# One broadcast read of reciprocal row sums, issued as two reads, one for each head of a pair

## The chip, the cores and the metric

The kernel runs on one core of one Trainium2 chip. The metric is the device time of the whole program in microseconds (us): for the kernel before, the median of 3 timed runs is 762.94 us (761.92 to 763.22). One further execution was profiled; its rows are the ones shown below.

## The reference

Two batches, eight heads, 768 tokens, head dimension 64. Each query and key is hashed to 6 sign bits by a shared projection; a query attends only to keys with the same bits. Two feed-forward layers with fixed weights (512 to 2048 to 512) follow, all in float32:

```python
mask = q_bucket[:, :, :, None] == k_bucket[:, :, None, :]
scores = np.where(mask, scale * np.matmul(q, k.transpose(0, 1, 3, 2)), -1e9)
attn = np.exp(scores - np.max(scores, axis=-1, keepdims=True))
attn = attn / (np.sum(attn, axis=-1, keepdims=True) + 1e-09)
x = np.matmul(attn, v)                       # then to [1536, 512]
h = x @ w_in;  x = where(h >= 1, h, where(h <= -1, 0, (h + 1)**2 / 4)) @ w_out
h = x @ w_in2; out = (h - np.tanh(h)) @ w_out2
```

## The kernel before

**Attention.** Heads are taken in pairs, and a pair's queries in two halves of 384 (`SH`). For a block of 128 queries TensorE writes the scores over 768 keys into PSUM (`emit_s`, L447 and L451, tile `ss`); VectorE takes the row maximum (L465) and two small scalars from it (L468, tile `sm`); ScalarE takes the exponential with its row sum (L469, tile `p`, sums in `ls`); `p` is split into two float16 parts (L474 to L476, tile `phl`), which SyncE's queue turns by DMA transposes into `pt` (L480). After the six blocks of a pair (three for each head), TensorE multiplies `pt` with the values into `pv` (L571). The result is not yet divided by the row sums.

**The division.** `pv` has the two heads' 64 output dimensions on its 128 partitions and the 384 queries along the row, while the row sums lie with the queries on the partitions. They have to be turned and repeated: row `rb[h*64+d, q]` must hold `1/sum` of head `h`, query `q`, for all 64 `d`. In the first batch TensorE does that by matmuls (L510, copied by L515). In the second batch (`if b:` in `scale_l`) it goes through memory: VectorE forms the reciprocals (L493, L495), TensorE turns them (L498) into 6 rows of 128, VectorE copies these to `rts` (L499), a DMA stores them as `rsum` in DRAM (L500, 3 KB), and another DMA reads `rsum` back with every head's 384 values repeated on 64 partitions (L502, 192 KB, tile `rb`). This happens 8 times, once for each pair and half of the second batch. Then `pv` is multiplied by `rb` (L578 on VectorE), and the product is split into two parts `xh` (L239) and `xl` (L245) for the first feed-forward layer.

**Feed-forward.** Units of matmuls (`mats`, L737; L725 for the last) take `xh` and `xl`, or `gh` and `gl` of the hidden layer, against weights `wh` and `wl`; `post` evaluates the results. The first batch's units are mixed into the second batch's attention. The second batch's first layer begins when its last pair is divided.

**What sets the order.** Every operation is registered with a plan, with the cells it reads and writes. A table (`SCHEDULE`, compressed text) gives the order in which all of them are issued and the engine where there is a choice. Each engine works through its own instructions strictly in that order. All DMAs, transposes included, are issued by SyncE (SP) one after another; the issue of one waits if its data or its buffer isn't ready, and everything behind it waits too.

The lines of the transfer in question:

```python
src = rsum[m].rearrange("j k p -> j (k p)").unsqueeze(1).to_broadcast([2, D, SH])
one("SP", 400.0, lambda: SP.dma_start(out=RB[0], in_=src), [("rs", m)], [("rb", 0), ("rb", 1)])
```

The outermost dimension of this source is the head (2), then the 64 repeats with step zero, then 384 contiguous values.

Of the kernel before, what the change touches and what calls it, by code (L numbers as in the profile page):

```python
# [22 lines left out]
SCHEDULE = (
    "c-rk)dvH|c6+h>D-siruo84qL31O3vm?sI@L_=N#LIS}MNGymTPahb;2Vy`$(J~fAp@^eGZO1az4z0D?q1Eaij-##4sMSuZwsf32YPJ2N9mkFx|Iq2V3(}Be"
    "^HAutGn`58y?ej&oyYIIzTKsRw=aP!5Y}DI-0POX^-)-Saqm{O$y8S`Erf#xGISANwz=XG+qj82s2$fea6MRaOuqyngL8lvmqmD(11p$r2SSj@L&%-uMhzCQ"
    "wS*=Ng_=UB^%o5ghOC^=K4rkSTk*(E7R1aDkNgwxZ~p067!0C5?oT8xhj(mMS;=1o&^+7%C3i%lS&|k0>iJyzc^1p#@)dyJ80Im=&bb;oqzizE4lLH#*w}~-"
    "tDvh39^eg-64~s0*e=S2D6ea5WVHx2b9G1Ut{L+{btJ)^Et{I4K(rP^>MEYBIUk1NaRyiyvubM-iD+(Bydqj&9<}22F(}Dyh@@(Y;*qN9sdzPnD~+s3cG-E6"
    "(qw5Q!ph65tEYu@a9T-TIGhX@g)QdCl0d)^!CXf}M4C>1z6=Hp9muh)5atHMVKWd3nZaNnWM*T;^_u}7`V*nWE`sB893`WX?9an-9?mjC*|AT!<}CRm>AJxn"
    "v)}_CBDn9l%8A7y>i$SXSpY%9@4wrxIP7J>OmG~O&H*J4;^xgJ8U}1*j0vTlhzSs3>*$~mz?fgkhd*=IeeQl&GTUCYV!cgVtOjmFDVN`(5tqsiuG-t%yOaXC"
    "opsEfEnZXVl@@WCd<n3=p08d#*ueS9TDD>hW6MA0D_ytZ$PtdFVVX=MTZs4HFNAvN;KA>x!-qOatN!9XHg_)^lymmTmb;zj91Ph3`#FlD@vQL});_iUNei*s"  # L30
    "*mlE_qeqORi2Sqf{gAHWnnPDVSi_}!P#8kIeV_XF2C?st;+;Rd@y0%--rl=ch_}?sFTd^s$pyUd0%ssrqCoy!06*q1_$;`;_!Nl#^0N;<`1>(aTwnk^t{#K;"
    "<k8t6-h5Mt+3;I<%VfsyfYKNnl!_^oFV+COq=1PRyV;AJ!!yrl&7NYvL;+?v903-JJPsHL;1~XsNWr77-yi(zKV1964=tbXqxXH5^)7$U=lkT{2mbuN?@!!1"
    "?l{~$e%t~@P^VZ{mbN&5?KS_a+}8hc97li1!9g2<A}u&RO~|81Li`wi|Kv}p5FdS=X~rChk63|_6%63h5BU%MI!Za=W>LwS2c%El1;SLOA<Z91*e{jZ@qjw8"
    "Q#=6sZ`NGF(6;amk_ESfgb<r<y^V41qnx^(EJ7+)4QiVpph%^-=o0KVjFOE8-^3{?w7$ZJ`9h+#hf>+HA_D9UK|rNeH#OeTpb%y*fqLFqUCn3CoEe&N<zTC>"
    "sM2k1dA#ca)eTK^o0{Z3jParrPqO@4SSAFP_aihDm9eri*27pyF+g#si1Yg9%5Wf%msQIB6%`e^oF_S4?Y6iDrAbNsCsh!KxWRLHtg<o+vp8?2lxD@1Gb9ux"
    "142wIDne0sc`}tkmPb10)H6&ZlqxUJE6B-fif6|VvXjXOgr{3oeO5j<{a`GZ##mG-7S3Thkgauv&!-1mp;$t)MT>;4f&$0VV5l4?$V}lg41-w&pcc8gb323+"
    "lP#@L9%_n2EKBf@lGIIu;QriSSy>6f4V1Zp%_)K6)?&siOXZ|eP%m`?XZa4+)z#GcAQt0Kik_aHK-pp<-~gQqZ|=mRF12+l$HKNYmm$cus}dXW%D7?3da1D1"
    "##O88>MjAZs)|?Qz|eI!uq`+A`;@x2v~=_4QqBjFEjVz1U7_`1A@=@c^)YcwtN~MTiuSHuckR+r${n{*Shovi96s#u2dNXNd!;^b;2O>Lf$Wedn8|TBu2c7}"
    "Ie@FFrx^F#GkD21!`O3Uz%cNeE<bpX^J6;&4n9T+Ou1w{^5}ZGd$-<mUE6K9?Ur)WrcILMsG%XXfB*h_EHpV2d-iMu($3jNWINf8eLEQ39b)3neRnb;IOmLA"
    "yBia?--5e#BIc-DZl<EV3AWz97-AP*zh%po;ziIS_N)xoLm{WCy$oR8T7Ye!ZX7Z}t&-O(2nVyI7;L6=hQ3mSg|KD~T@)1Ba{2Ok)8Vr9?QCrXuo>2_bz~hZ"  # L40
    "@B|@bWi4(u;Z@$l<suNm?r!XA95DMkFJ?=YRO_Pt{!N=9Z%NxleSJO6Q~@Zgd6!};#aHlfR9i+n7_AJJHDA~Ov4ymMek4|7CKBynBX!;zjq^2)9^fLCqGEGl"
    "2Iea_s{(^E2BIXpxHxV?KH+MbIp;BqPLl`<4aQ<i6wdbL&hSYYO{(d(9S+MZ8UTT^GF3WF^I|S%PIq}I6mt^P355*lha>j1q|TBdInChyc--;(bF?k&r4dzV"
    "UCE=N9?<bXAS9ykIJ8TMwHw^g=J^~9^!x2Zf}Hoq{QhjTEXNUzw$?r^oPq*J1%pA0Cuzbk-GtI;gnZZ4b@|cynU)=+(h0SjW)fg?p{aKp9@W{lX=KMM<3>DE"
    "MxV1oGC!Y8Qw8&P&iDIGnLWfbDKHtM-52;$-*Ouo>fH@<>ldVUcF$QmYks@d<ujXIeeJbYPfv?x&FZQn4O-vcXw7+XR{J5#`bMiZYnHNVuo}_qF-59-)-2xH"
    "y`EZX=dxw1R;{LT9T*ru=99Pfqa*BMabc0@?xysZ={TEqbvXU~PUZJ2`<$VhHaJ@^HGSYNw7~3wfdR1A4p_`oD_6EtELxvv?QUsVpj2Pyyvua&rE`_Kq-TXv"
    "s*B5kb#lPp@29{owd~&B-bLFsQpKAK%x>PZ#<njt7Ob?eYkptf+K!H1rrLW@wzc;5O1V_dgT?dbUI5hjp^b=USW^>kZ%KFQdY9&uAQP~Xv01ZNRTYTRQsPx5"
    "bP6k_S}!bMNt*S7#q(HhZb3l-HN_~kbDCWc%z|h%1fg)q4`5q9r1O(Ol>pwq^6JpFEGbRXpu++J1IwaQ04nOz94(+zp%%(}MiW4Q*M$jH#b_il+6<bxoD16F"
    "jSonZ@J0y<p~^?jt@IL06Dg!w<H>R8uxZkWqtOjCw@qS}-sn!7MY@quMRH=o6Dm3Put|?aptFte$kSz{*T_+lK^qAa&pd6?S%gXOc&Xu0S1}}Y7RmzpoR&nY"
    "JdKQd=btnXB*+F0NZnPE+2k+X$*eRAv;dL`uYaPq?zK9an`9;tl_~eY_Dloq*+nnSllX%t2)#`*{nj8ar7O`s0U5oeEp*;SuhJFuJ~A^cm7z{!K~{NidaT3?"
    "RCa<qBQ~!Bh46{A1>`!pK)nULJRrRUoo5l5=!M18l}6PQl@5XT?8R1iQ6j9UohdqU(Kga`0@1WN9&vJ=7`31S0<EP1^`ygzSlYyDFfUA=GW0Tsdq|`gIi~G^"  # L50
    "w953&!yD+h>Nwzdcfc>7PTpZ+az@-oeso5z+9z-J2toF#r7s_bUx)G8!&dCk>!YMjY0aK+*O{RSHQ<@mXQlt9Ksf4p7RdY>e&du_5GT0{$9jP$-(yC@@f72i"
    "4CWNE7@^oWbs3wC({3YQkGF;H#>vYl4&#i3)fhv#F)0)OON9U9^3KsYXwMFba}b=Pb99dWANoF?ex@309N^i|dse*pY6n}yGi*Cfif=NfWt_wZJk1ZB<oAuQ"
    "<mhP-pZKml)$j}xftex0uag8gu}?U)nBtT|Gj@=M`HxdEZXC6la$ua@I64*ZE9b)aDTR}*9vs(Fz=;9E46ft2RXO>5!?D<LGS1+Cz7^wSTM16m>r+BUWHXN2"
    "38$Fs6U)w!M3}iq@bnntSLltWcN3giL&MBPia2hajj|0VPJl^f9gYMJCzq)>a)KjH=r(3T9j8*9I7%E&zUapZNG6YQg1(ItsGV@mPcS)fvLgT|S4-m~Fd=}W"
    "Qx(VdCBtC{aX8P&AMY|dd)nN`jPf#JI=ZwGGldvOXJ)3u>DYE)CctnE0b@Lk3GQ$JFmr#y%q;@PjLvYq6Tvo?iI|}ajGREDey7E;Ou;e0I7{?zk;J4U"
)


# [866 lines left out]
```

## Time and profile before

| | |
|---|---|
| timed runs | 762.94 us median, 761.92 to 763.22, 3 runs |
| profiled execution | 766.08 us, of which the span from first to last instruction is 764.2 us |
| TensorE (PE) busy | 739.8 us, 97% of the span |
| VectorE (DVE) busy | 543.0 us, 71% |
| ScalarE (ACT) busy | 450.9 us, 59% |
| GpSimd (POOL) busy | 344.5 us, 45% |
| mean granted TensorE clock | 0.993 |

How to read it: TensorE is busy nearly all the time, so the other engines' shares matter only where they make TensorE wait. An idle time is told with what ended it: "PE ss L447 <- ACT p L469" is TensorE standing before line 447 until ScalarE had finished line 469. The granted clock is 1.00 at TensorE's full 2.4 GHz and 0.50 at 1.2 GHz. The part of the span that belongs to the second batch's attention runs to about 494 us; behind it there are only feed-forward units.

### The profile page before, as it was taken

The numbers are of one execution on the slowest core, as the hardware profiler recorded it, in microseconds if no ns is written. First come the engines' busy times: TensorE is split into PE (matmuls) and PEld (weight loads), VectorE is DVE, ScalarE is ACT, GpSimd is POOL, SyncE is SP. The second block draws the span as 40 slices with busy tenths as digits, with TensorE's granted clock in tenths as the row PEclk, the third lists the DMA queues.
The fourth block names the chain that finished last, engine by engine and source line by source line (L and its number), as shares of the span: only waits on it lengthen the run. The fifth ranks groups of instructions, "written<-read, shape, count | busy, mean of one in ns | idle before, by whom it ended". The sixth has DMA issues, their size and how long they took to land. (4 is left out here: it accounts for less than half of the span.)

```text
span 764.2 us, 12558 instructions
## 1 busy us (share of the span) xinstructions
PE 739.8 (97%) x4608; PEld 685.9 (90%) x4608; DVE 543.0 (71%) x958; ACT 450.9 (59%) x728; POOL 344.5 (45%) x229
## 2 busy tenths in 40 slices
PE   7899999989999999999999998899999999999997
PEld 6666789768989999999999997799999999999997
DVE  7999988879888888987888895352633555253653
ACT  8998898878879688766775575052423324221110
POOL 6974465665646356555444576222013322231220
PEclk9999999999999999999999999999999999999999
DMA  6996886999999998997988867431221221122212
GB/s 191 212 283 232 204 254 233 222 214 249 246 226 235 198 207 205 269 212 212 232 226 222 198 165 127 121 111 58 81 69 56 69 69 56 56 59 67 69 41 83
DMA packets 164861, 124.97 MB, mean 164 GB/s; under 512 B 126864, under 2 KB 134848, under 8 KB 164800
## 3 DMA queue, kind: packets, MB, share of 16 engines
q1 hardware_dynamic: 164800, 124.18, 64.7%
q8 instruction: 36, 0.59, 0.3%
q14 instruction: 25, 0.20, 0.1%
HBM read 73.53 MB, written 19.95 MB: 122 GB/s over the span
## 5 line engine op out<-in xcount | busy, mean ns | idle before, releaser
L245 POOL TENSOR_TENSOR wl<-wr,wh 128x512 fp32r<-128x512 f32 x77 | 107.1, 1393 | 176.0 <-ACT wh L239 71.9
L737 PE MATMUL mm<-xh,wh 128*128 128x384 f32 x512 | 137.5, 339 | 1.8 <-DVE xh L239 1.8
L737 PE MATMUL mm<-xl,wh 128*128 128x384 f32 x512 | 136.3, 336 | 0.5 <-POOL xl L245 0.5
L737 PE MATMUL mm<-gh,wh 128*128 128x384 f32 x504 | 136.4, 341 | 0.0
L737 PE MATMUL mm<-xh,wl 128*128 128x384 f32 x512 | 136.1, 336 | 0.0
L737 PE MATMUL mm<-gl,wh 128*128 128x384 f32 x504 | 133.9, 336 | 0.0
L737 PE MATMUL mm<-gh,wl 128*128 128x384 f32 x504 | 133.9, 336 | 0.0
L475 POOL TENSOR_TENSOR phl<-p,phl 128x768 f16<-128x768 f32 x46 | 80.7, 1755 | 73.5 <-ACT phl L474 39.4
L245 POOL TENSOR_TENSOR gl<-tmp,gh 128x768 fp32r<-128x768 f32 x35 | 68.0, 1945 | 93.0 <-DVE gh L239 58.6
L469 ACT ACTIVATE p<-ss,sm 128x768 f32<-128x768 f32 x78 | 77.2, 989 | 39.7 <-DVE sm L468 37.0
L737 PEld LDWEIGHTS mm<-xh,wh 128*128 128x128 f32 x512 | 92.7, 189 | 4.0 <-DVE xh L239 2.1
L737 PEld LDWEIGHTS mm<-gh,wh 128*128 128x128 f32 x504 | 90.9, 189 | 4.0 <-issue 2.0
L737 PEld LDWEIGHTS mm<-xl,wh 128*128 128x128 f32 x512 | 93.4, 188 | 1.0 <-POOL xl L245 0.8
L239 ACT ACTIVATE wh<-wr 128x512 fp32r<-128x512 f32 x88 | 54.7, 625 | 66.1 <-PE mm L737 60.0
L737 PEld LDWEIGHTS mm<-xh,wl 128*128 128x128 f32 x512 | 93.6, 189 | 0.0
L465 DVE TENSOR_REDUCE sm<-ss 128x1 f32<-128x768 f32 x82 | 78.2, 954 | 20.6 <-PE ss L451 18.2
L737 PEld LDWEIGHTS mm<-gl,wh 128*128 128x128 f32 x504 | 92.1, 189 | 0.0
L737 PEld LDWEIGHTS mm<-gh,wl 128*128 128x128 f32 x504 | 92.1, 189 | 0.0
L246 DVE TENSOR_TENSOR wl<-wr,wh 128x512 fp32r<-128x512 f32 x67 | 50.4, 755 | 24.2 <-ACT wh L239 23.1
L787 DVE TENSOR_TENSOR accs<-mm,accs 128x768 f32<-128x768 f32 x45 | 43.0, 954 | 34.4 <-PE mm L737 34.1
L756 ACT ACTIVATE tmp<-mm,cb 128x768 f32<-128x768 f32 x32 | 28.8, 899 | 52.6 <-PE mm L737 52.6
L760 ACT ACTIVATE tmp<-mm 128x768 f32<-128x768 f32 x32 | 25.9, 809 | 53.7 <-PE mm L737 48.7
(179 smaller groups left out, 1235.0 us busy)
## 6 DMA issues: line engine op xcount, KB each, us to landing
w<-in_w SPq DMA_DIRECT2D x64, 512.0 KB
qr<-in_qT SPq DMA_DIRECT2D x32, 192.0 KB
wr<-scr0i SPq DMA_DIRECT2D x24, 256.0 KB
wr<-scr0o SPq DMA_DIRECT2D x24, 256.0 KB
krs<-in_kT SPq DMA_DIRECT2D x14, 384.0 KB
vr<-in_v SPq DMA_DIRECT2D x12, 384.0 KB
scr0i<-wr SPq DMA_DIRECT2D x16, 256.0 KB
scr0o<-wr SPq DMA_DIRECT2D x16, 256.0 KB
```

What stands on the lines that cost most here:

```text
L239: ways = [("A", ca, lambda: A.activation(dst, src, AF.Copy)), ("V", cv, lambda: V.tensor_copy(dst, src), 1)]
L245: op([("G", cg, lambda: G.tensor_tensor(dst, src, hi.bitcast(F32), op=ALU.subtract)), ("V", cv, lambda: V.tensor_tensor(dst, src, hi.bitca ...
L246: ("V", cv, lambda: V.tensor_tensor(dst, src, hi.bitcast(F32), op=ALU.subtract), 1)], reads, writes)
L465: one("V", 870.0, lambda: V.tensor_reduce(z[:, 0:1], s, axis=AX.XY, op=ALU.max), cell, [c])
L469: one("A", 970.0, lambda: A.activation(halves(p), s, AF.Exp, bias=z[:, 2:3], scale=z[:, 1:2], accum_out=LS[lm][:, lk:lk + 1]), cell + [c], ...
L475: lo = [("G", 1600.0, lambda: G.tensor_tensor(hl[:, S:2 * S], p, hl[:, 0:S], op=ALU.subtract)), ("V", 870.0, lambda: V.tensor_tensor(hl[:, ...
L737: T.matmul(ps[:, s + hf, 0:SH], m[:, kc * 128:(kc + 1) * 128], y[:, hf * SH:(hf + 1) * SH], start=(kc == 0 and i == 0), stop=(kc == 3 and ...
L756: one("A", 690.0, lambda: A.activation(halves(t), ps, AF.Relu, bias=half_b, scale=0.5), [pc], [c])
L760: one("A", 690.0, lambda: A.activation(halves(t), ps, AF.Tanh), [pc], [c])
L787: one("V", 870.0, lambda: V.tensor_tensor(a, ps, a, op=ALU.add), [pc], c)
```

## The change

The read at L502 becomes two reads, one for each head. Each has 64 partitions of `rb` as its destination and, as its source, the head's 384 values with 64 repeats as the outermost dimension. Each writes one of the two cells `rb`. The plan gets 8 operations more, and the table is written anew for their number.

```diff
 SCHEDULE = (
-    "c-rk)dvH|c6+h>D-siruo84qL31O3vm?sI@L_=N#LIS}MNGymTPahb;2Vy`$(J~fAp@^eGZO1az4z0D?q1Eaij-##4sMSuZwsf32YPJ2N9mkFx|Iq2V3(}Be"
...
+    "c-rk)d2pRo*?*qrtnYf?yXGeMCTWsp>6WBPnuUg}lr{@(x{zQ?TLKoaB@`@`E-ba8LKjgBYAb372bDoZ)IrC=QD<;O9lmcwM^SMZT+s0kN5*l+@nb&EdlR8e"
...
-                src = rsum[m].rearrange("j k p -> j (k p)").unsqueeze(1).to_broadcast([2, D, SH])
-                one("SP", 400.0, lambda: SP.dma_start(out=RB[0], in_=src), [("rs", m)], [("rb", 0), ("rb", 1)])
+                for h in range(2):
+                    src = rsum[m][h].rearrange("k p -> (k p)").unsqueeze(0).to_broadcast([D, SH])
+                    one("SP", 400.0, lambda h=h, src=src: SP.dma_start(out=RB[0][h * D:(h + 1) * D], in_=src), [("rs", m)], [("rb", h)])
```

SyncE's queue near the seventh and the eighth of these reads, before (`wr` are weights, `scr` their copies in DRAM, `out_T` the output):

```order
L685 DMA scr1o_245<-wr_119 128x512
L502 DMA rb_102<-rsum_161 128x1x384
L480 DMA_TRANSPOSE pt_108<-phl_106 128x12x128
L480 DMA_TRANSPOSE pt_109<-phl_107 128x12x128
L480 DMA_TRANSPOSE pt_109<-phl_106 128x12x128
L659 DMA wr_119<-scr0i_185 128x512
L480 DMA_TRANSPOSE pt_109<-phl_107 128x12x128
L500 DMA rsum_162<-rts 6x128
L792 DMA out_T<-accs 256x1x384
L659 DMA wr_118<-scr0i_184 128x512
L502 DMA rb_102<-rsum_162 128x1x384
L659 DMA wr_116<-scr0i_186 128x512
```

The same place after (lines below the edit have moved by one):

```order
L686 DMA scr1o_245<-wr_119 128x512
L503 DMA rb_102<-rsum_161 64x384 x2
L480 DMA_TRANSPOSE pt_108<-phl_106 128x12x128
L480 DMA_TRANSPOSE pt_109<-phl_107 128x12x128
L480 DMA_TRANSPOSE pt_109<-phl_106 128x12x128
L660 DMA wr_119<-scr0i_185 128x512
L480 DMA_TRANSPOSE pt_109<-phl_107 128x12x128
L500 DMA rsum_162<-rts 6x128
L793 DMA out_T<-accs 256x1x384
L660 DMA wr_118<-scr0i_184 128x512
L503 DMA rb_102<-rsum_162 64x384 x2
L660 DMA wr_116<-scr0i_186 128x512
```

The second read stands right behind the first; nothing else has changed its place, here or at the other six reads. On TensorE, VectorE, ScalarE and GpSimd the instructions stand in the same order as before.

## Rows read from the trace of the kernel before

**Rows 1.** Page, part 1; then the chain of waits: start, us, what.
```profile
PE 739.8 (97%) x4608; PEld 685.9 (90%) x4608; DVE 543.0 (71%) x958; ACT 450.9 (59%) x728; POOL 344.5 (45%) x229
...
494.69 261.01 PE mm L737 x1491
```

**Rows 2.** Waits over the span: total us, times, longest us.
```profile
DVE rb L578 <- DMA rb<-rsum: 9.8, 4, 4.3
...
PE ss L447 <- ACT p L469: 5.6, 8, 2.2
...
PE mm L737 <- DVE xh L239: 1.8, 1, 1.8
```

**Rows 3.** Four stretches: length, busy us and count by engine, clock, DMA share, GB/s.
```profile
230.00:470.90 240.90, 240.89 (x1487) 229.87 (x1485) 203.27 (x351) 170.76 (x281) 133.01 (x85) 1.00 0.90 210
473.19:477.64 4.45, 4.45 (x16) 4.45 (x17) 3.13 (x6) 2.86 (x5) 2.50 (x2) 0.62 0.38 71
493.61:498.00 4.39, 3.93 (x12) 3.60 (x13) 1.56 (x3) 1.75 (x2) 2.24 (x2) 0.61 0.01 4
498.00:755.70 257.70, 257.70 (x1483) 256.49 (x1483) 123.69 (x161) 74.59 (x97) 65.45 (x42) 1.00 0.22 67
```

**Rows 4.** Timeline at the seventh read: start, us, instruction, count, [idle before <-releaser].
```profile
466.91 0.96 DVE L465 TENSOR_REDUCE sm<-ss 128x1 f32<-128x768 f32 x1 [2.91 <-PE ss L451]
...
470.46 0.51 PE L737 MATMUL mm<-gh,wl 128*128 128x384 f32 x2
...
471.09 0.56 DVE L578 TENSOR_TENSOR rb<-pv,rb 128x384 f32<-128x384 f32 x1 [3.23 <-DMA rb<-rsum]
...
472.06 0.99 ACT L469 ACTIVATE p<-ss,sm 128x768 f32<-128x768 f32 x1 [5.57 <-DVE sm L468]
...
473.19 0.62 PE L447 MATMUL ss<-ak,aq 128*128 128x384 f32 x2 [2.22 <-ACT p L469]
```

**Rows 5.** Timeline at the eighth read.
```profile
485.25 0.55 SPq L502 DMA_DIRECT2D rb<-rsum  x1
...
487.92 0.43 DVE L239 CAST wh<-wr 128x512 fp32r<-128x512 f32 x1 [1.69 <-DMA wr<-scr0i]
...
491.46 0.34 PE L737 MATMUL mm<-xh,wh 128*128 128x384 f32 x1
492.61 0.56 DVE L578 TENSOR_TENSOR rb<-pv,rb 128x384 f32<-128x384 f32 x1 [4.26 <-DMA rb<-rsum]
...
493.61 0.44 PE L737 MATMUL mm<-xh,wh 128*128 128x384 f32 x1 [1.81 <-DVE xh L239]
493.64 1.00 POOL L245 TENSOR_TENSOR xl<-rb,xh 128x384 fp32r<-128x384 f32 x1 [9.62 <-DVE xh L239]
...
494.69 0.69 PE L737 MATMUL mm<-xl,wh 128*128 128x384 f32 x1 [0.46 <-POOL xl L245]
```

**Rows 6.** Stretches of the clock, columns as in rows 3.
```profile
156.65:159.95 3.30, 3.30 (x21) 1.72 (x22) 2.81 (x6) 2.10 (x5) 1.64 (x1) 0.50 0.89 208
474.05:477.40 3.35, 3.35 (x12) 3.35 (x11) 3.06 (x5) 1.89 (x5) 2.50 (x2) 0.50 0.37 70
494.55:497.90 3.35, 3.21 (x10) 3.21 (x11) 1.46 (x3) 1.75 (x2) 1.32 (x2) 0.50 0.00 0
```

**Rows 7.** DMA issues: sizes.
```profile
rb<-rsum SPq DMA_DIRECT2D x8, 192.0 KB
```

**Rows 8.** Stretches in which one transfer moves most of the bytes, columns as in rows 3.
```profile
468.00:469.00 1.00, 1.00 (x8) 1.00 (x7) 0.00 (x0) 0.00 (x0) 1.00 (x2) 1.00 0.14 40
469.00:470.00 1.00, 1.00 (x8) 1.00 (x7) 0.00 (x0) 0.00 (x0) 0.47 (x1) 1.00 0.15 41
478.00:479.50 1.50, 1.50 (x10) 1.50 (x10) 0.75 (x2) 0.74 (x1) 0.00 (x0) 1.00 0.86 215
```

**Rows 9.** SyncE's issues: one by one at the seventh read; then min/median/max ns.
```profile
464.44 0.55 SPq L502 DMA_DIRECT2D rb<-rsum  x1
465.09 4.09 SPq L480 DMA_TRANSPOSE pt<-phl  x1
...
L502 SPq DMA_DIRECT2D rb<-rsum x8: 541/546/1429, 218.2 to 485.2; - x8
...
L480 SPq DMA_TRANSPOSE pt<-phl x72: 1274/1628/4881, 20.0 to 479.8; - x72
```

More of the change, by code (lines that the diff above doesn't have):

```diff
@@ L23 @@
 SCHEDULE = (
-    "c-rk)dvH|c6+h>D-siruo84qL31O3vm?sI@L_=N#LIS}MNGymTPahb;2Vy`$(J~fAp@^eGZO1az4z0D?q1Eaij-##4sMSuZwsf32YPJ2N9mkFx|Iq2V3(}Be"
-    "^HAutGn`58y?ej&oyYIIzTKsRw=aP!5Y}DI-0POX^-)-Saqm{O$y8S`Erf#xGISANwz=XG+qj82s2$fea6MRaOuqyngL8lvmqmD(11p$r2SSj@L&%-uMhzCQ"
-    "wS*=Ng_=UB^%o5ghOC^=K4rkSTk*(E7R1aDkNgwxZ~p067!0C5?oT8xhj(mMS;=1o&^+7%C3i%lS&|k0>iJyzc^1p#@)dyJ80Im=&bb;oqzizE4lLH#*w}~-"
-    "tDvh39^eg-64~s0*e=S2D6ea5WVHx2b9G1Ut{L+{btJ)^Et{I4K(rP^>MEYBIUk1NaRyiyvubM-iD+(Bydqj&9<}22F(}Dyh@@(Y;*qN9sdzPnD~+s3cG-E6"
@@ L28 @@
[L28 to L55, printed above, removed]
+    "c-rk)d2pRo*?*qrtnYf?yXGeMCTWsp>6WBPnuUg}lr{@(x{zQ?TLKoaB@`@`E-ba8LKjgBYAb372bDoZ)IrC=QD<;O9lmcwM^SMZT+s0kN5*l+@nb&EdlR8e"
@@ new lines @@
+    "a+8}1j?DDjd*An*_nh;b-?N<Ociy}0w&U;?+zWg5lXpn%ghMG98y8pJp>Gp(voATJA|JnxuI9-41hR~U7_nUMdWB#QTEZ6~qJztURVP`30acYdnE<i~nf?;5"
+    "Tt`Vkr<<@awmOCi+C&l(q8RBFei-ab@~{nQE5;!44}3XNi51Z(s@)OD{OTpAq+YII7W@!;k_>9zTT~P$V2hqDw!iaTq*Mmjb3f7e^~=|44IsQ;Am&3SjA+32"
+    ";dX4>4(s47YlBvvq7FF3m+|E-9Uat+1dW%e{-*nC*FcZ#s{-M!UJd2EyBb>ev8u)nIFiW_U~@~_Zps#wG-Ov46)#&>WVdG0P?Ks)HZE?-B<m|P4UlMBq2tNa"
+    "lBLPIWW1tA$7xA@eOWY7Q(m3Lns{X#m&CNsBXRJhNZZ1TTcR`?&FDx_Y{zXZi6*Rgkc?T;AZ|rcnDio6;A12k8}Sfa-<5)_R3iC*@e+!sV@d_7ztCcOOn5Ob"
@@ new lines @@
+    "N;dq?NAQ0Oo-B6LN%`Sq5`+a&9f_QbNCqbe$hW{n;hvG=A>3=B2DO_VAfZS;!6C&HkJ&eIt|1_LSp40)?iKIjf}EXv*EZYcv=S8Ik*!CBLb=&EU-rJUcR<Q+"
+    "5Y*Y%$^S<_E4%ph;+ZyrYggUOu3@c=u3ouqoVLEq{q5u}|0F}}tgVSjJR@-M!<@^HJ@7I4(5W+g4F~n$8e%6voa(zzbe(j+>0-<Y9Q+1a_>}$}HhuLFK4D>l"
+    "KDZwre)M7W=s%Es;xov_t$1eQbR!euG}rv6A5tH@p1+^}jQ`*l&;Q_l`O}l~1b<$A?>YWm9|Ys@G$Z&H-+?B2zZu|P7~J#}cwhM&fP4wQWWjHK^QB8PJpK}V"
+    "UVaw3Ulh*+|1rOm!*lQxi}a7cDn)2VSu9a}dnLd#5{Q4}=@ELG!Bd(PeU-k39PC6<0w|Vx954v*|07+z3%pN7A}{~R3;yW*!S?+>{?51U7uj!p|F188<oAyE"
@@ new lines @@
+    "!Y`Tq>z_Lgd%*@tL~Rsjk_GyIBkWm6ecyFoan+w0pyL>%1e)R3KnUbS_&DcZ#uu3NIDY1NgTNz!pSFXTjX~sFACG+W8B77Xwi9*ml<-f2F}k+25c;zp1R>>J"
+    "XXV|e`C0hLor*~~c>BSGpy>V>=eO{Cj}ePR5ZOHv$!Kq)<uLGY{c#}x^_5#{^&ZXC%?yQ7Z}YK?3+K2~j5b)ilPvCPdMn8L`g>%z97Sk?R<^d0H8)Q*G{x#C"
+    "den*r)my^`dslbM0qE@P7xxpf>New`%Ce>g7-I~!bT0$y+_aRIbWkl|bxSR<Snp!iS|3d`v!FB{)UIHxm{ry71;3(eX|)07RPfd;WLc9gVa4@nSj9Q8PFBn6"
+    ">uM!LMWvuci}#31T3o@(STiF*jlC_UN@dCxEiEl6Eh(x7fK*iqnnvw-d3pUJdxOoaN*^?l%u*r|OB-XXP!Z*gdVI5_tf2K=)kC>!t1M{gMQw_3Qi@B97?&j_"
@@ new lines @@
+    "-0e^I^av+)DT}UVaf_KW$bTONFVfHe*%kZ=FS^v@)L&Z*UUxOQirU+uxK*Iau8KU^(z3ES0>yH}hS>6=;Z3knz`*)}BglsC7&=>Xhz)>bm8=KAfzDpBXHOR2"
+    "meHbBNNg6@;LesEEh}wkU{}>^d^>H~zi*$v55=u@b$jb*!bH&SQ-kz@PpBKX9RI=z{-k)4kK4-ZM|Je5I3bUi7!eN(=T3oiK!22-aZWSaR`h^4b&I0+OXv^7"
+    "&|>%=l-E8mehRHqJ56S}`hACQ()!qe;9iZ2yAQGl*pqj2oNyUFW+UoP?|QF(L>%9D&pr2wZh6aIahDMzAKZQLl(au^|Lrz1I(}RMBYwjKA-$9Crn~Mp87y&<"
+    "(=q-&&KSL$?nS&cd*oes^lmIcdF0MCiaX%;(}zk%V8d<uYu4|BE86+7?NG%K@J0adI=B`NgFJW$#!blXH&m5K2p*Z>og9{IG^2(9#>a<Xr-TYeY+X|cH|*-A"
@@ new lines @@
+    ">yqGOCtNF<uK_+7%7S?R#^>S|uwZxt12N1m;R79`*4i!GXmg_)8@qKQRF!U?xT<#(Z5+OINFwJp?rdYN$!$!f!0NM955ZfyHndAf4*_4dD7Dfr>raOp+XT-6"
+    "lVsXKa$Z4^7HFnAC~u4?jH7@^QEd^guFinQ(mF?FY_$Z_Xtt$96P{^_8~u{ib-qYf3t8njA|A(>1;Ns#a!G|^HB2;Bd0DeJ%S4oMF5>Eulv|+^qN2)<2^M6t"
+    "UcgI~<6h~eRHd_<EwW<6DTpRSkj_G;PeO5@<y#Kt9X10fFLx4tsqgW?<-VVAJal=Wbc?SRCAch&am!-9#zhKE!np+6%RJ?_lohqwk;b*Qo$^!^^xLbBfmLCt"
+    "c5Q3dw(N9iL#d^+DJ`m0jY_F#ytMMD2-Zc{29_u~NXk_X$)L+h1d%qnuf5f8y?#w=+u)I1gZ-=4^=Z9acdc~X?qR)`1|OYJm$u)e-=m$&o@rmz_mH#I>CyJe"
@@ new lines @@
+    "E2$Bj4z$<Xt)g{s6~AWP(5@W-Y~9wKjBn>-bakM%jFB(Ntq~*D;(&<@#+oj7-MvT0E^`~UJmR{C-Q^>@4q5Nm37$7>Qr=YqFbei{qc&M`N1t)V)}HP!b`Qv|"
+    "LAhz|<u|I4@ikKJki%C?Il#o&E-@C22Ea#MZ`0<HJ2!H74>|U*J+zChx14bYheo&GXb%jm*|bKF5cXZ64AovGH>~TrVh}bCfP(%G!|Hv!tGnAU6z}Wi5%SxF"
+    "*DZwM5o%zXtzygSml>K`W)g&`6>O<dqLP&_rYb5Yb2iIl5z7&v2$IF7nSx{t(($51G!Ah9H*m-|sZfJ7S80w_GNe$KYt6MHCd@`4v?MBl<{)Uo!7^?}VW<_%"
+    "7SSdsh50eCNg8635Ym+)H$=<)Afyt&Fm!=Hp%H=1$b)bl2HfB?%r796LEzw2gPD{twGMI?LIRHF3>V&V;tT_rnpwwC)Ra6!0A?snVv@jejepgF$l#MXc%TiP"
@@ new lines @@
+    "nbg9y8Dq$Zg>6HNpt(Y$FENM0rDRSq$M^tEk~O+d$qN?`(V31=1+XMjW|F~y8pBxz15K$1IcO%&<{*SxPd+u%wK<)HN!2#bO)WRy0wXjOz)+edQb<N7JDRfs"
+    "3JTkkwg9jJCx@E4MTTdLB@Bkis?Wj+p)8hjO(-J76v{AS)oXT~vg*G^8ebb&l8c;C!)gu~g=;Y}se?fmS{ZW=$iWMP3}5xoBtXaXX_|7AaXb&>MMG|Bv(BW`"
+    "rUZpX$<1_K7jhrh9A<L0u<A}$V7}r`yH9VqGrHZWt20fKbN&;@d97pGxL5nayE7*|XMugryt7`PGVcob`mSf^zJ(W@aeae|eW7~ef`%X#Gz({chEqMSbz3tA"
+    "oj<^uF=D~`=-fAN(dS&JKb>>Rq+mVUP_17VpX%9!>p~FzhYJ4J3%pn^+V+hq{GtgimW$<Ld9!4HoVw0I3U3ld#|u5+BEHVpv7m8<oSLzK2A-z}7Wm?EL5iMd"
@@ L56 @@
+    "Vno1&yXPDcnBQdh?*swPuM;lJr??>3%<iOf^v8vOn`7C0F)+t$ys&prypY#eEOh(eoKOMhw-Dyh9p~JZg$EqYYI-b08+`5k7z<4%SfJXk3Y`|uIA<<gV7SjO"
+    "8}mrT{QCsY_cC5UdOSa&;KFhm&aqJu=iF;Ez~THMP+;KU49j6*(TdY)9C2R7F`wOWAsciSd06<)pUWqCRK|I-H_o^0ymUVgfncFbfQ4bgxot4731@~Y&aO<J"
+    "Ll5G)W2XO^mtWiS_#gAi%V*S?`x`NzlW}Hn<~yX$jsx=<3}+EAOKn!;o@)TipX4xqn!s7TbMCtHnQb<Rm?sfT=b;(@+v03ca28{{LFJzfyQNP"
 )
```

## The prediction

> **What bounds the kernel now.** I read the page's busy shares first, then the chain of waits, then the list of waits, then the timeline wherever TensorE waits late. TensorE is busy for 97% of the span, and the chain that ended last is TensorE alone from 494.69 us on [rows 1]. So a microsecond is worth something only where TensorE stands still or runs slowly. Four stretches show where that is [rows 3]. From 230 to 470.9 us it is busy for 240.89 of 240.90 us, and from 498 to 755.7 us for all 257.70 us. Between these lie two places where it waits, and both hang on the transfer that is changed.
>
> The list of waits has VectorE waiting four times, 9.8 us in all and at most 4.3, for the read of `rb` [rows 2]. Two of the four reach TensorE.
>
> *Place A, the seventh read.* VectorE is done with L465 at 467.87 us and stands before the multiplication L578 until 471.09, 3.23 us, for the read [rows 4]. Queued behind L578 on VectorE are the two scalars of the next softmax (L468); ScalarE waits 5.57 us for them before the exponential at 472.06, and TensorE, whose only score tile is still being read, waits 2.22 us and resumes at 473.19.
>
> *Place B, the eighth read.* Issued at 485.25, it lets VectorE begin L578 at 492.61 after 4.26 us of idleness [rows 5]. TensorE reached the first-layer unit that needs the result at 491.63 (its last start, 491.46, plus one matmul), gets `xh` at 493.61 and `xl` at 494.69: it is idle for 1.81 and 0.46 us.
>
> *The clock.* Behind each of these waits the granted clock is 0.50, that is 1.2 GHz instead of 2.4, in rows of 3.35 us [rows 6], although TensorE is fully busy again. It then loses time with no idle time to show for it.
>
> What A and B cost with this slow stretch: the usual pace is 257.70 us / 1483 = 0.1738 us a matmul [rows 3]. A: without the wait the next matmul would have started at 470.46 + 2 x 0.174 = 470.81; the pace is normal again at 477.64, and 16 matmuls lie between [rows 3, 4]. 6.83 us were spent on 16 x 0.1738 = 2.78: 4.05 us lost. B: from 491.63 to 498.00, 6.37 us for 12 matmuls, 2.09: 4.28 us lost [rows 3, 5]. Together 8.33 us.
>
> **The change, part by part.** *The read itself.* It moves 192 KB [rows 7], 196,608 bytes. While it is nearly alone, in the two stretches from 468 to 470 us, the DMA engines are busy for 0.14 and 0.15 of their time and move 40 and 41 GB/s [rows 8]: 0.145 x 16 is 2.3 engines. The source before has the two heads as its outermost dimension, and it seems to be spread by that: one engine a head. At 40.5 GB/s the bytes take 4.85 us. A load whose outermost dimension is the 128 partitions shows 0.86 and 215 GB/s [rows 8]; at that rate they take 0.91 us. No transfer with 64 repeats outermost stands in this trace, so I bound it: at best the rate of the 215 GB/s row, at worst the read finishes later than now (the slower rival below). I take the 215, since 64 rows of the same 1536 bytes are the same kind of packets over as many engines, and a repeat of one row is already read now at 20 GB/s an engine without a fault. The gain is 4.85 - 0.91 = 3.94 us.
>
> *The second issue.* An issue of this read takes SyncE 0.546 us [rows 9], so the second half starts about 0.55 us later. The data is complete 3.94 - 0.55 = 3.39 us earlier.
>
> *What is late next at A.* 471.09 - 3.39 = 467.70, before VectorE is free at 467.87: its wait is gone. TensorE's wait needs only 2.22 of that. The multiplication, the scalars and the exponential all move forward by 3.2 us, the exponential to 468.9, and TensorE wants the score tile at 470.81. The 2.22 us and the slow clock go: 4.05 us.
>
> *What is late next at B.* All of B's chain starts with a matmul of TensorE's own (L498), so it moves with TensorE, and I compare inside the old times. 492.61 - 3.39 = 489.22; VectorE is free at 488.35 (the cast of `wh`) [rows 5]. `xh` is there 1.00 us after L578 begins and `xl` after 2.08 (493.61 and 494.69 against 492.61): 490.2 and 491.3. TensorE wants them at 491.63 and 0.35 later. The wait is gone with 0.7 us to spare: 4.28 us. If only 2.7 us were gained, not 3.4, `xl` would begin to be late.
>
> *Eight more issues on SyncE.* 8 x 0.546 = 4.4 us of its queue. At the first six reads TensorE is covered: it has no idle time between 230 and 470.9 us. Behind the seventh a DMA transpose takes SyncE 4.09 us to issue against a median of 1.63 [rows 9], while the 2.3 engines work; the transposes are spread over all engines and seem to stand behind the read on the two it uses. This jam should end, so SyncE gains more at each read (up to 2.5 us) than the second issue takes. If it doesn't end, 0.55 us is late for each transpose behind; nothing of that reaches TensorE before 470.9 us. I count it as zero.
>
> *The sum.* 766.08 (the profiled execution, 1.9 us beyond its span) - 8.33 = 757.75. The median of the timed runs is 762.94, 0.4% below the profiled one; scaled alike, 762.94 x 757.75 / 766.08 = 754.6. I say 754.7 us.
>
> A rule speaks against the change. The Trainium skill, in "DMA: Bandwidth & Descriptors", section "Rules for kernel authors", says of two transfers to disjoint halves of the partitions not to bother, since both spread over all 16 engines and follow one another. By it the sum would be zero gain, or a little less than zero for the second issue. The trace doesn't meet its premise: the one transfer uses 2.3 engines, not 16. The same section tells that a leading repeat of c copies confines a transfer to c engines, which is what 0.145 looks like.
>
> **The rivals.**
>
> 1. *One of the two waits stays.* For: the timed runs are 3.1 us shorter than the profiled one, and no row says where; it could be that A or B with its slow clock is shorter in them. At B two stores of the output share the engines, and 0.7 us isn't much. Against: A has 1.2 us of reserve, B moves as a whole. Only one is won: 762.94 - 4.2 = 758.8.
>
> 2. *The waits go, the slow clock doesn't.* There is a third slow stretch, at 156.65 us, in a place that the change doesn't touch [rows 6]. If the clock fell near A and B for what the stretch does at large, or falls elsewhere instead, only 2.22 + 1.81 + 0.46 = 4.5 us are won: 758.4. Against: from 230 to 470.9 and from 498 to 755.7 us, where nothing waits, the clock is 1.00 throughout [rows 3].
>
> 3. *It does not do what it says.* The halves still go by few engines, or follow one another as the rule has it. Each half then takes 2.4 us, the second starts 0.55 us later, the end comes between as late as now and 0.55 us later at A and B: 762.9 to 764.0, 763.3 as its time. Against it stands only the share of 0.145.
>
> 4. *Slower: sixteen engines on one row.* Now two engines read two different rows of 1536 bytes over and over, 20 GB/s from each. Afterwards all engines of a half read one row at once. If the memory yields no more than these 20 GB/s from one row, each half takes 98,304 bytes / 20 GB/s = 4.9 us, the second behind the first, and the data comes about 4.9 us later than now; A and B grow by that each: 762.9 + 9.8 = 772.7. It decides as soon as a row yields under 40 GB/s. Nothing in the trace shows a row read by more than one engine, for or against.
>
> **How the numbers follow.** Forecast 754.7: 0.52. Rival 1: 0.20. Rival 2: 0.12. Rival 3: 0.08. Rival 4: 0.05. The remaining 0.03 is a gain above 10 us, by transposes freed earlier. About 0.2%, 1.5 us, is what a measurement of this kernel can tell from no change, so everything but rivals 3 and 4 is "faster": 0.87; same 0.08; slower 0.05. The forecast alone, with 0.7 us for a late `xl` and the spread of the runs (1.3 us), reaches from 753.2 to 756.5. Rivals 1 and 2 (758.4 to 758.8) belong in the range, rivals 3 and 4 stay out: 753.0 to 760.4.
>
> **What would show it right or wrong.** In the profile after: VectorE's waits for `rb` fall from 9.8 to under 2 us; TensorE has no idle time of over 0.3 us between 230 and 750 us; both stretches at 0.50 near A and B are gone; the transpose behind the seventh read is issued in under 2 us; the DMA share during a read is far over 0.15. Wrong it is if VectorE still waits 3 us for `rb`; if TensorE waits at A or B for something else (the last transposes before L571, a weight at 487.92); or if the rows show the waits gone and the time does not follow.

## The result, and the profile after

The changed kernel takes 754.2 us (median of 4 runs, 753.85 to 754.38) against 763.08 us (4 runs, 761.92 to 764.77). The ratio is 0.9881, with an interval of 0.9862 to 0.9900: 9.1 us less, between 7.6 and 10.5. The forecast was 754.7 us.

The profiled execution took 753.85 us with a span of 752.1. The page's busy shares and the chain of waits, which answer to [rows 1]:

```profile
PE 733.2 (97%) x4608; PEld 681.9 (91%) x4608; DVE 538.5 (72%) x958; ACT 450.2 (60%) x728; POOL 345.3 (46%) x229
...
480.32 263.24 PE mm L738 x1512
```

TensorE's unbroken run to the end now begins right behind the last `pv` product instead of behind a wait. The list of waits, against [rows 2] (the multiplication with `rb` is L579 now):

```profile
PE ss L447 <- ACT p L469: 2.8, 6, 1.1
DVE rb L579 <- DMA rb<-rsum: 1.4, 1, 1.4
```

Of four waits for the read, 9.8 us, one of 1.4 is left, and TensorE's wait for `xh` is no longer in the list. Stretches of the trace, columns as in [rows 3]:

```profile
200.00:460.00 260.00, 260.00 (x1618) 248.45 (x1618) 224.25 (x394) 190.41 (x317) 141.74 (x90) 1.00 0.86 215
460.00:500.00 40.00, 40.00 (x248) 38.47 (x249) 19.66 (x33) 16.00 (x22) 16.21 (x11) 1.00 0.61 154
500.00:743.00 243.00, 243.00 (x1399) 241.79 (x1398) 116.00 (x154) 66.24 (x87) 60.45 (x39) 1.00 0.21 61
```

From 200 to 743 us TensorE is busy without a gap and the granted clock is 1.00 throughout; places A and B lie in the middle stretch. The timeline at the seventh read, against [rows 4] and [rows 9]:

```profile
460.50 1.10 SPq L503 DMA_DIRECT2D rb<-rsum  x2
461.69 1.46 SPq L480 DMA_TRANSPOSE pt<-phl  x1
...
463.03 0.96 DVE L465 TENSOR_REDUCE sm<-ss 128x1 f32<-128x768 f32 x1 [2.98 <-PE ss L451]
463.90 0.55 DVE L579 TENSOR_TENSOR rb<-pv,rb 128x384 f32<-128x384 f32 x1
...
466.93 0.51 PE L447 MATMUL ss<-ak,aq 128*128 128x384 f32 x2
```

VectorE goes from L465 straight to the multiplication, and TensorE to the score matmul without a bracket for idle time. The issue of the transpose behind the read takes 1.46 us instead of 4.09. Over all transposes the issue takes, min/median/max in ns as in [rows 9]:

```profile
L480 SPq DMA_TRANSPOSE pt<-phl x72: 1275/1482/3354, 19.7 to 472.6; - x72
```

The timeline at the eighth read, against [rows 5]:

```profile
477.28 1.14 SPq L503 DMA_DIRECT2D rb<-rsum  x2
...
481.87 0.56 DVE L579 TENSOR_TENSOR rb<-pv,rb 128x384 f32<-128x384 f32 x1 [1.43 <-DMA rb<-rsum]
...
482.90 1.01 POOL L245 TENSOR_TENSOR xl<-rb,xh 128x384 fp32r<-128x384 f32 x1 [6.85 <-DVE xh L239]
...
483.85 0.56 PE L738 MATMUL mm<-xl,wh 128*128 128x384 f32 x2
484.25 0.51 PE L738 MATMUL mm<-xh,wl 128*128 128x384 f32 x2
```

VectorE still waits 1.43 us, but TensorE doesn't. It is a narrow thing: `xl` is finished at 483.91, and the pair of matmuls that needs it stretches from 0.51 to 0.56 us. The read itself, against [rows 8]. Its packets are those of 1536 bytes in the trace, one for each of the 128 rows of `rb`. Before, the first of the seventh read starts at 465.85 us and the last at 470.65; after, at 461.86 and 463.38, 1.52 us instead of 4.80. Two half microseconds in which nearly all bytes are the read's:

```profile
462.00:462.50 0.50, 0.50 (x5) 0.50 (x4) 0.00 (x0) 0.50 (x1) 0.21 (x1) 1.00 0.47 141
462.50:463.00 0.50, 0.50 (x5) 0.50 (x4) 0.00 (x0) 0.05 (x1) 0.37 (x1) 1.00 0.66 189
```

Instead of 40 GB/s it gets 141 and 189. On how many engines a read goes is in the trace's semaphore records: the semaphore that the seventh read raises as its data lands goes up in two steps before, at 471.02 and 471.07 us (besides one jump at 465.41, before its first packet), and in 16 steps for each half after, the last at 463.84. At the other seven reads the numbers of steps are the same.

**Where the time came from.** The turn of the reciprocals (L498) stands in TensorE's order once before each read, so the stretches between these turns hold the same work in both traces. Before (first, seventh and last of eight; columns as in [rows 3]):

```profile
204.97:238.92 33.95, 33.47 (x208) 31.42 (x207) 29.05 (x55) 26.45 (x48) 18.14 (x12) 1.00 1.01 213
...
455.90:482.87 26.97, 24.75 (x150) 22.92 (x149) 16.54 (x28) 12.68 (x21) 14.28 (x10) 0.94 0.79 145
482.87:764.20 281.33, 275.01 (x1586) 271.18 (x1584) 129.91 (x172) 76.34 (x99) 68.84 (x45) 0.99 0.23 70
```

and after:

```profile
202.62:235.79 33.17, 33.17 (x209) 31.43 (x208) 28.62 (x55) 26.52 (x48) 18.08 (x12) 1.00 0.97 222
...
452.06:474.91 22.85, 22.85 (x151) 21.42 (x150) 16.20 (x28) 12.55 (x20) 14.30 (x10) 1.00 0.69 161
474.91:752.10 277.19, 273.09 (x1586) 269.80 (x1584) 128.40 (x172) 76.32 (x99) 68.93 (x45) 1.00 0.24 71
```

A: 26.97 - 22.85 = 4.12 us. B: 281.33 - 277.19 = 4.14. The six stretches of the first six reads: (455.90 - 204.97) - (452.06 - 202.62) = 1.49, of which 0.78 in the first. Together 9.75 us. The traces of the kernels below agree on these six: from the first turn to the seventh it is 250.8 to 251.8 us in the five that have the old form there ("before", "seventh", "eighth", "last2", "filled"), and 249.4 to 249.6 in the three that have the new form ("after", "change_again", "first6").

The spans differ by 12.1 us; the other 2.35 lie before the first turn (204.97 against 202.62), where nothing was changed, and come and go between executions: in the kernel "doubled" below, with the old reads, that turn starts at 202.5 us. One difference there is the slow stretch at 156.65 us of [rows 6]: the trace after has none before its first turn.

### The profile page after: what moved, and what is told of

Its sections match the earlier page's. It is cut to its first block, busy times and chain, and to the rows that moved or that the text cites. A ratio compares the mean times of both kernels' runs of the same rounds, so it can differ in the third digit from the quotient of the medians.

```text
span 752.1 us, 12578 instructions
## 1 busy us (share of the span) xinstructions
PE 733.2 (97%) x4608; PEld 681.9 (91%) x4608; DVE 538.5 (72%) x958; ACT 450.2 (60%) x728; POOL 345.3 (46%) x229
## 4 chain that ended last, share of the span: by engine, by line
PE 78%; DMA 1%; DVE 1%; ACT 1%; issue 0%; POOL 0%; SPq 0%; ACTq 0%; DVEq 0%
PE mm L738 66%; PE pv L572 4%; PE ss L447 3%; PE ss L451 2%; DMA pt<-phl 1%; PE mm L726 1%; ACT p L469 1%; DVE sm L465 0%; PE pb L338 0%; PE pb L352 0%; PE pb L353 0%; PE pb L339 0%; PE pv L562 0%; POOL phl L475 0%; PE pb L367 0%
## 5 line engine op out<-in xcount | busy, mean ns | idle before, releaser
L465 DVE TENSOR_REDUCE sm<-ss 128x1 f32<-128x768 f32 x82 | 78.3, 955 | 23.8 <-PE ss L451 22.2
```

The source lines that it names most:

```text
L465: one("V", 870.0, lambda: V.tensor_reduce(z[:, 0:1], s, axis=AX.XY, op=ALU.max), cell, [c])
```

## Experiments

All are compared with the kernel before. Microseconds are (1 - ratio) x 763.1. Where an edit applies to some reads only, both forms stand in one operation of the plan and the order is that of before. "last2", "wide16_again" and "change_again" (the changed kernel once more) were timed side by side, as one group.

### Parts of the change: the first six reads, the seventh, the eighth, the last two

```diff
-one("SP", 400.0, lambda: SP.dma_start(out=RB[0], in_=src), ...)
+
+def read():
+    if g // 2 - 2 * NP < 6:          # "first6"; "seventh": == 6; "eighth": == 7; "last2": >= 6
+        for h in range(2):
+            one_head = rsum[m][h].rearrange("k p -> (k p)").unsqueeze(0).to_broadcast([D, SH])
+            SP.dma_start(out=RB[0][h * D:(h + 1) * D], in_=one_head)
+    else:
+        SP.dma_start(out=RB[0], in_=src)
+
+one("SP", 400.0, read, ...)
```

> The two-read form for the first six of the eight reads, the one-read form for the last two; order of all other work as before. Theory S (the read is slow because only about two DMA engines carry it, and only the waits behind the seventh and eighth read reach TensorE): no gain, 763.1 within 0.8 us; TensorE waits of about 2.2 and 1.8 us stay, both stretches at clock 0.50 stay. Rival J (what is won is the DMA queue: transposes no longer jam behind each read, at all eight places): a gain of about six eighths of the whole, 756 to 758 us.

> The two-read form for the seventh read alone. Theory S: the wait of 2.22 us at about 473 us and the slow clock behind it go, worth 4.05 us: 759.0, with the eighth read's wait and slow clock as before. Rival J: one eighth of the gain, 762. If the slow clock did not hang on the wait: 2.2 us, 760.9.

> The two-read form for the eighth read alone. Theory S: the waits of 1.81 and 0.46 us and the slow clock behind them go, worth 4.28 us by the prediction's sum: 758.8, with the seventh read's wait and slow clock as before. Rival J: one eighth of the gain, 762. If the slow clock did not hang on the wait: 2.3 us, 760.8.

| kernel | median us | ratio, interval | us won |
|---|---|---|---|
| first6 | 761.89 | 0.9957, 0.9933 to 0.9982 | 3.3 (1.4 to 5.1) |
| seventh | 761.04 | 0.9949, 0.9926 to 0.9973 | 3.9 (2.1 to 5.6) |
| eighth | 760.27 | 0.9947, 0.9916 to 0.9978 | 4.0 (1.7 to 6.4) |

The seventh and the eighth behave as forecast, 4.05 and 4.28, though each interval is about 4 us wide. In the timeline of "seventh", from 465 us on, TensorE's only waits before the last unit are those of the eighth read:

```profile
490.16 0.44 PE L746 MATMUL mm<-xh,wh 128*128 128x384 f32 x1 [1.71 <-DVE xh L239]
491.24 0.44 PE L746 MATMUL mm<-xl,wh 128*128 128x384 f32 x1 [0.46 <-POOL xl L245]
```

Three stretches of it: the one of A between the turns of L498, a part behind the eighth read where the clock is down, and the one of B (columns as in [rows 3]):

```profile
456.67:479.51 22.84, 22.84 (x150) 21.41 (x149) 16.12 (x28) 12.53 (x20) 14.30 (x10) 1.00 0.73 165
491.90:495.20 3.30, 3.30 (x12) 3.30 (x11) 2.44 (x3) 2.02 (x3) 0.52 (x1) 0.50 0.19 38
479.51:760.80 281.29, 275.12 (x1586) 271.28 (x1584) 130.13 (x172) 76.30 (x99) 68.81 (x45) 0.99 0.23 70
```

The stretch of A is as short as after the change (22.85), that of B as long as before (281.33). In "eighth" it is the other way round, in the timeline and in the same stretches:

```profile
472.46 1.01 PE L447 MATMUL ss<-ak,aq 128*128 128x384 f32 x2 [2.10 <-ACT p L469]
```

```profile
455.33:482.03 26.70, 24.60 (x150) 22.85 (x149) 16.14 (x28) 12.52 (x20) 14.27 (x10) 0.94 0.78 144
472.30:475.60 3.30, 3.14 (x10) 3.15 (x11) 2.17 (x4) 1.88 (x5) 1.68 (x2) 0.50 0.12 25
482.03:759.40 277.37, 273.28 (x1586) 269.75 (x1584) 130.17 (x172) 76.34 (x99) 68.82 (x45) 1.00 0.23 71
```

"first6" misses the expectation: it is clearly faster, where nothing was expected. Rival J's 5 to 7 us are not reached either, and both waits at the last two reads stand as before. A part of the cause is in the timeline of the kernel before, just ahead of a stretch that the prediction began at 230 us:

```profile
226.00 0.56 DVE L578 TENSOR_TENSOR rb<-pv,rb 128x384 f32<-128x384 f32 x1 [0.91 <-DMA rb<-rsum]
226.69 0.76 ACT L679 ACTIVATE wr<-w,cb 128x512 int32<-128x512 uint16 x1 [1.95 <-issue]
...
227.40 0.21 DVE L468 TENSOR_SCALAR sm<-sm 128x1 f32<-128x1 f32 x1
227.91 0.98 ACT L469 ACTIVATE p<-ss,sm 128x768 f32<-128x768 f32 x1
...
229.03 0.62 PE L447 MATMUL ss<-ak,aq 128*128 128x384 f32 x2 [0.48 <-ACT p L469]
```

The first read makes TensorE wait as well; in "seventh", "eighth" and "filled", which read it in the old form, it is 0.6 to 1.1 us. One cause is the chain of A: VectorE's wait for `rb` makes its scalars (L468) late, which are ready at 227.61. The other is that ScalarE begins the exponential only at 227.91, behind conversions of weights (L679, L678) that stood still until 226.69: at most 0.3 of the 0.48 us. By the trace's semaphore records, ScalarE waited there for a store of a weight tile `wr` that SyncE had issued behind the read, at 219.05. Of this store's 16 steps 14 were done by 223.0 us, the last two came at 226.61 and 226.62, after the read had landed on its two engines (225.98). After the change the same store is complete at 222.33 and ScalarE goes on to its L679 without idle time. So a read on two engines also delays what is queued behind it. What all six reads are worth was put to a test beside the change itself:

> The two-read form for the seventh and eighth read, the one-read form for the first six. The trace of the kernel before shows the first read reach TensorE too (0.48 us of idleness at 229 us) and stretches between the turns of the reciprocals (L498) longer than in the changed kernel by 1.5 us in all up to the seventh. Theory S as corrected: this is the whole change without that 1.5 us, 1.3 to 2.0 us slower than the change, some 756 us; a wait at 228 to 230 us stays, those at the last two reads are gone. Theory S as predicted (the first six reads are worth nothing): the same as the change, 754.2 to 754.7.

"last2": 756.82 us, ratio 0.9908 (0.9885 to 0.9931). The change in the same group: 754.60, 0.9880 (0.9857 to 0.9903). The difference of 2.2 us is a little over the 1.3 to 2.0 of the corrected theory and speaks against zero, though the two intervals overlap. In its timeline TensorE's wait at the first read is there, and those at the last two are gone:

```profile
227.34 0.62 PE L447 MATMUL ss<-ak,aq 128*128 128x384 f32 x2 [1.01 <-ACT p L469]
```

### Split without spread, spread without split

In "columns" each read is two transfers, but the two heads stay outermost:

```diff
-one("SP", 400.0, lambda: SP.dma_start(out=RB[0], in_=src), ...)
...
+for c in range(2):
+    cols = slice(c * SH // 2, (c + 1) * SH // 2)
+    src = rsum[m].rearrange("j k p -> j (k p)")[:, cols].unsqueeze(1).to_broadcast([2, D, SH // 2])
+    SP.dma_start(out=RB[0][:, cols], in_=src)
```

> All eight reads as two transfers, but divided by columns: each covers all 128 partitions and 192 of the 384 values, with the two heads still outermost. The split alone, without the spread. Theory S: the DMA share during a read stays near 0.15 of 16 engines, the data comes as late as before or later by the second issue and by smaller packets (0.5 to 1.5 us), so 763 to 767. Rival T (it is the splitting that helps: two transfers under way at once, each with its own completion): the gain of the change, 754 to 756.

768.57 us, ratio 1.0050 (1.0022 to 1.0077): 3.8 us slower (1.7 to 5.9), at the upper end of what was expected. Each transfer's semaphore goes up in two steps, as with one read. The list of waits has 14.3 us of VectorE's for the read instead of 9.8:

```profile
DVE rb L583 <- DMA rb<-rsum: 14.3, 4, 5.2
```

and in the timeline TensorE's wait at A has grown from 2.22 to 3.40 us:

```profile
475.88 0.62 PE L447 MATMUL ss<-ak,aq 128*128 128x384 f32 x2 [3.40 <-ACT p L469]
```

In "wide16" the read stays one transfer and is spread by other means; "wide4" has NR = 2 and so 4 rows:

```diff
+NR = 8
-rsum = bufs("rsum", 2, [2, TPH, 128], F32, dram)
+rsum = bufs("rsum", 2, [2, NR, TPH, 128], F32, dram)
...
+rep = ls[:, 2 * TPH:].rearrange("p (j k) -> p j k", j=2).unsqueeze(2).to_broadcast([128, 2, NR, TPH])
+one("V", 70.0, lambda: V.reciprocal(LR[m].rearrange("p (j r k) -> p j r k", j=2, r=NR), rep), ...)
...
-src = rsum[m].rearrange("j k p -> j (k p)").unsqueeze(1).to_broadcast([2, D, SH])
+src = rsum[m].rearrange("j r k p -> (j r) (k p)").unsqueeze(1).to_broadcast([2 * NR, D // NR, SH])
```

> One read for each pair, spread over the engines by other means: the reciprocals are written eight times into a 48-column tile, turned by one transpose into 48 rows, stored as 16 rows of 384 (24 KB), and one read takes these 16 rows, 8 repeats each, with the 16 rows outermost. The spread alone, without the split. Theory S: the same waits go as with the change, 754.2 within 0.8 us; without the second issue the data comes up to 0.5 us earlier still, which nothing waits for. Rival T (the split is what helps): 763. If many engines reading one row cost something in the change, this is faster than it by that.

> As the one with 16 rows, but with 4 rows of 384 outermost and 32 repeats each: the read should go by 4 engines, about 2.4 us instead of 4.85. Theory S by the prediction's margins (2.22 us needed at the seventh read, 1.9 us for xh and 2.9 us for xl at the eighth): the waits go but for some 0.5 us, the clock stays up, 754.5 to 756. If a gain in transfer time is passed on only in part: 758 to 760. Rival T: 763.

> The one read of 16 rows again, now beside the change. Theory S: the same as the change within 0.8 us, since in both no wait for the reads reaches TensorE any more. If sixteen engines on one row had a price, or the second issue, this would be faster by it.

> The changed kernel beside the other two of this group, on the same chip: 754.2 us, 0.988 of the kernel before.

| kernel | median us | ratio, interval |
|---|---|---|
| wide4 | 756.32 | 0.9903, 0.9887 to 0.9918 |
| wide16 | 755.32 | 0.9904, 0.9885 to 0.9923 |
| wide16_again | 754.25 | 0.9874, 0.9850 to 0.9897 |
| change_again, same group | 754.60 | 0.9880, 0.9857 to 0.9903 |

The first time "wide16" lies above its expected 754.2 within 0.8 us; beside the change it gives what the change gives. The two cannot be told apart, so there is no version here that beats the change. Rival T is out by both tests. The number of engines follows the outermost dimension: the read's semaphore goes up in 16 steps with 16 rows and in 4 with 4. A stretch of "wide4" inside its second read shows 0.26 of the 16 engines, four of them, at 99 GB/s (columns as in [rows 3]):

```profile
251.00:252.00 1.00, 1.00 (x7) 1.00 (x6) 1.00 (x2) 0.63 (x1) 0.07 (x1) 1.00 0.26 99
```

"wide4" ends 0.3 us above its expected range. Its eighth read comes later than with 16 rows, and a small part of the wait at B is back, without the slow clock: a rest of 0.60 and 0.46 us of the 1.81 and 0.46, in the timeline of "wide4":

```profile
483.83 0.56 DVE L585 TENSOR_TENSOR rb<-pv,rb 128x384 f32<-128x384 f32 x1 [2.88 <-DMA rb<-rsum]
484.84 0.44 PE L744 MATMUL mm<-xh,wh 128*128 128x384 f32 x1 [0.60 <-DVE xh L241]
485.92 0.44 PE L744 MATMUL mm<-xl,wh 128*128 128x384 f32 x1 [0.46 <-POOL xl L247]
```

### The slow clock by itself

```diff
+for _ in range(32):                       # ahead of L447 of the last block: place A
+    T.matmul(WT, warm, warm, start=True, stop=True)
...
+if u == last_wait and kc == 3 and i == 0 and hf == 1:
+    for _ in range(28):                   # between two matmuls of L737: place B
+        T.matmul(WT, warm, warm, start=True, stop=True)
```

> The reads as before; TensorE is given 32 dummy matmuls (128 columns, about 0.055 us each, 1.8 us in all) just ahead of the score matmul that waits behind the seventh read, and 28 (1.5 us) between the two matmuls between which it waits behind the eighth. They lie inside the waits and shorten none. Theory S with the clock as its second term: the waits' ends stay where they are, the stretches at 0.50 behind them go, worth 4.05 - 2.22 - 0.2 and 4.28 - 1.98 - 0.46, together about 3.4 us: 759.7. If the slow clock comes from something else than the standstill: 763.1 and the two stretches stay.

"filled": 761.02 us, ratio 0.9968 (0.9954 to 0.9983), 2.4 us won (1.3 to 3.5); 3.4 were expected, and between the turns of L498 its trace is 1.52 us shorter at A and 1.51 at B. VectorE waits for the read as before (10.5 us in all), and the clock is up. Two stretches, columns as in [rows 3], first in the kernel before:

```profile
472.00:478.00 6.00, 4.81 (x19) 4.81 (x20) 4.28 (x8) 4.05 (x8) 2.50 (x2) 0.72 0.60 118
490.50:497.00 6.50, 4.23 (x17) 3.58 (x16) 2.35 (x4) 0.91 (x2) 2.24 (x2) 0.81 0.07 24
```

and then in "filled":

```profile
472.00:478.00 6.00, 5.49 (x38) 5.32 (x36) 4.18 (x8) 4.10 (x8) 2.51 (x2) 1.00 0.61 119
490.50:497.00 6.50, 5.85 (x47) 5.35 (x45) 3.55 (x5) 2.16 (x3) 2.24 (x2) 1.00 0.14 39
```

What is left of TensorE's waits in its timeline:

```profile
473.06 0.62 PE L447 MATMUL ss<-ak,aq 128*128 128x384 f32 x2 [0.51 <-ACT p L474]
491.88 0.45 PE L746 MATMUL mm<-xh,wh 128*128 128x384 f32 x1 [0.19 <-DVE xh L239]
492.96 0.45 PE L746 MATMUL mm<-xl,wh 128*128 128x384 f32 x1 [0.46 <-POOL xl L245]
```

So the standstill makes the clock fall here, and the fall costs about a third of what A and B cost together.

### Twice the bytes on the two engines

```diff
+IDLE = bufs("idle", 1, [128, SH], F32)
-lambda: SP.dma_start(out=RB[0], in_=src)
+lambda: (SP.dma_start(out=IDLE[0], in_=src), SP.dma_start(out=RB[0], in_=src))
```

> Each read is preceded by another of the same form into a tile that nobody uses: the same two engines carry twice the bytes, and the wanted half comes second. Theory S: the data comes 4.85 + 0.55 = 5.4 us later at both places, TensorE's waits grow by as much each, and earlier reads may begin to reach it too: 763.1 + 10.8 = 773.9, or a few us more. If much of the wait were latency that two transfers share: under 768. Rival T or J has no number for it, except that the queue jams longer.

"doubled": 788.78 us, ratio 1.0333 (1.0314 to 1.0353), 25.4 us slower. More than twice what was expected, and the trace shows where. Earlier reads reach TensorE with long waits, the first with 4.62 us, and near the reads the clock falls at four places instead of two. Between the turns of L498 the first six stretches grow by 16.8 us, A by 3.8 and B by 3.2. At A the wait of VectorE grows by less than 5.4, from 3.23 to 6.93 us. From its timeline:

```profile
230.69 1.01 PE L448 MATMUL ss<-ak,aq 128*128 128x384 f32 x2 [4.62 <-ACT p L470]
...
489.17 0.56 DVE L579 TENSOR_TENSOR rb<-pv,rb 128x384 f32<-128x384 f32 x1 [6.93 <-DMA rb<-rsum]
```

Two stretches behind the seventh read's issue, columns as in [rows 3]:

```profile
484.00:485.00 1.00, 1.00 (x7) 1.00 (x6) 0.00 (x0) 0.00 (x0) 0.00 (x0) 1.00 0.13 48
485.00:486.00 1.00, 0.34 (x2) 0.02 (x1) 0.00 (x0) 0.00 (x0) 0.00 (x0) 1.00 0.13 48
```

In both, all packets that start are the reads', but for two of 4 bytes. The share is 0.13, two of 16 engines, at 48 GB/s; at that rate 196,608 bytes take 4.1 us. In the first stretch of [rows 8], with 40 GB/s, single packets of the read took up to 0.43 us, here at most 0.08; why was not settled.

## Why the prediction was right

- *The bound, and that the gain lies at A and B*: right. 4.12 and 4.14 us by the traces against 4.05 and 4.28; each alone, on the clock of the timed runs, 3.9 and 4.0.
- *The read goes by two engines because the heads are outermost, and the spread helps, not the split*: shown by "columns" (1.0050, two steps of the semaphore), "wide16" (0.9904 and 0.9874, 16 steps), "wide4" (4 steps, 0.26 of the engines) and the 0.13 of "doubled". The prediction's 2.3 engines are two.
- *Rival 3* is refuted: at A the read's rows start within 1.52 us instead of 4.80. The Trainium skill ("DMA: Bandwidth & Descriptors", "Rules for kernel authors") advises against two transfers to disjoint halves of the partitions, because both halves spread over all 16 engines. That premise does not hold here, where the undivided read uses two. The same section of the Trainium skill says that an outermost dimension of size c under 16 confines a transfer to at most c engines. The traces agree: two engines for c = 2 and four for c = 4.
- *3.39 us earlier*: at A the packets of the read take 1.52 us instead of 4.80, 3.28 less, and the data was there before VectorE came, at most 3.4 us after the first issue against 6.65. At B it came 4.59 us after the issue (481.87 - 477.28) instead of 7.36: 2.77 earlier, 0.6 less than forecast. By the prediction's own margin of 2.7 us that is the edge, and 0.05 us of it shows in TensorE's row. What the two neighbouring stores of the output had to do with it was not tried.
- *The first six reads count as zero*, and *two of the four waits for the read reach TensorE*: wrong. The six are worth 1.49 us by the two traces, and three of the four waits reach TensorE. Of the 1.49 us, 0.48 was an idle time of TensorE at 229.03 us; the stretch that was read as "no idle time" began a microsecond behind it. Another 0.30 lies in the same stretch between two turns, the remaining 0.71 in the other five, and where that arises wasn't settled.
- *The sum*: 8.33 us forecast, 9.75 by the traces, 9.1 (7.6 to 10.5) by the timed runs. The missing term is the one above. So it is in part luck that 754.7 came within 0.5 us of the measured 754.2: the sum lacked some 1.5 us, and the timed runs can't tell 8.33 from 9.75.
- *The jam on SyncE*: as forecast at the seventh read, where the issue of the transpose behind it falls from 4.09 to 1.46 us; the longest of all falls only from 4.88 to 3.35. What the jam costs TensorE was counted as zero; at the first read the store described above shows that transfers behind the read can matter. How much of the gain that is was not shown: no experiment parts it from the faster read.
- *Rival 1* is refuted by "seventh" and "eighth" (both parts win), *rival 2* by the trace after, with a clock of 1.00 from 200 to 743 us, and by "filled". *Rival 4* did not come: the seventh read's last step comes 3.34 us after its first issue with 16 steps on each of two rows of 1536 bytes, and 3.19 us in "wide16", with one issue and 16 rows.
